# TensorE's order tied to the program's from the first step on, transposes included, with new places for chunk 2's attention

## The chip, the core and the metric

The kernel runs on one core of one Trainium2 chip. The metric is the device time of one execution in microseconds (us); lower is better. TensorE is called PE in the profile (its weight loads PEld), VectorE DVE, ScalarE ACT, GpSimd POOL and SyncE SP.

## The reference

Windowed attention over 8 sequences of 576 positions with 8 heads of 64, then a feed-forward network over the 4608 tokens:

```python
scores = scale * np.matmul(q, k.transpose(0, 1, 3, 2))      # scale = 1/8
mask = (rel >= 0) & (rel < 64)                              # rel = query - key
attn = softmax(np.where(mask, scores, -1e9))
x = np.matmul(attn, v)                                      # -> 4608 x 512
h = x @ w_in                                                # 512 -> 2048
g = h * np.tanh(log1p(exp(h)))
out = g @ w_out                                             # 2048 -> 512
```

## The kernel before, in words

The 4608 tokens are 12 chunks of 384 columns. Each chunk has an attention part for 4 pairs of heads, and a feed-forward part of 16 steps f.

The attention of one pair has three units on PE. **S**, the scores (`att_scores`): 12 small matmuls into two banks `s_ps`, one for each head. DVE then takes the masked minimum (L150), ACT the exponential (L153), DVE divides by the sum (L161 to L163) and `pr` is ready. **T**, the transposes (`att_transpose`): for chunks 0 to 3, two times three PE transposes of `pr` into `t_ps`, which ACT and DVE copy to `pT` (L185); from chunk 4 on DVE and DMAs do this, and PE has no T. **O**, the values (`att_values`): 12 small matmuls into `o_ps`, from which ACT and DVE make the split x (`xh`, `xl`, L205 and L206).

One feed-forward step of chunk c, written (c,f), is an **h unit** (12 matmuls into `h_ps`, of which there are two buffers), then min, Exp, Square, Ln, Exp and a product on DVE (L223, L233) and ACT, then `gh` and `gl` (POOL, and ACT for chunk 0), and two steps later an **acc unit** of 9 matmuls (`ffn_out`). A buffer of `h_ps` is free again when L233 has read it.

While chunk 0 runs, the weights are loaded and split into high and low parts (`load_w`, two calls after each step of chunk 0): L273 and L279 on ACT, L276, L277, L278 on DVE, L274 and L280 shared between DVE and POOL. The buffers `wa` of this work and `t` of the feed-forward steps share one ring of four.

The steps: first (0,0) to (0,7), then (0,8), (1,0), (0,9), (1,1) and so on to (0,15), (1,7), then (1,8) to (1,15), then the chunks 2 to 11 one after the other. The attention of chunk c+1 is set among the steps before its own by `plan`, which gives each S, T and O a place counted in half steps. `run` emits what has come due.

What sets the order on each engine is a scheduler that goes by the order of the program, by priorities (`tc.high_priority`) and by its own estimate of when things are ready. `in_order()` limits it: while it is active, each PE instruction that its block emits must stand behind the last PE instruction recorded in `order`, so that blocks follow one another on PE as they are written. It works only when `ordered` is not empty.

Of the kernel before, what the change touches and what calls it, by code (L numbers as in the profile page):

```python
# [27 lines left out]
def tile_window_attn_mish_ffn(  # L28
# [10 lines left out]
    nc = tc.nc  # L39
    NPAIR, _, NT = qT.shape  # L40
# [6 lines left out]
    NM = NB // 2  # L47
# [12 lines left out]
    ident = const.tile([P, P], F32, name="ident")  # L60
# [13 lines left out]
    for j in range(2):  # L74
        m = const.tile([P, P], F32, name=f"mask{j}")
# [16 lines left out]
    order = []  # L92
    ordered = []
# [4 lines left out]
    def in_order():  # L98
        return tc.issue_after(order[-1]) if ordered else nullcontext()
# [6 lines left out]
    def bank(c, p, name):  # L106
        if c == 2 or (c == 0 and p % 2 == 0):
            return ps_acc.tile([P, CH], F32, name=name, tag=next(sums))
        return ps_at.tile([P, CH], F32, name=name, tag="at")
# [56 lines left out]
    def att_transpose(c, p, pr):  # L166
        pT = next(pTs)
        if c > 3:


            moved = []
            tr = ap_.tile([P, P // 32, HM, 32], F32, name="tr", tag="pr", bufs=2)
            nc.vector.transpose(tr.rearrange("p k j i -> p j k i"),
                                pr.rearrange("p j (k i) -> p j k i", i=32))
            for r in range(0, P, 32):
                for k in range(0, P, 32):
                    if 0 <= k - r % BLK <= BLK:
                        moved.append(nc.sync.dma_start(pT[k:k + 32, r // 32, :, :], tr[r:r + 32, k // 32, :, :]))  # L178
            return pT, moved
        for h in range(2):  # L180
            t_ps = (bank(c, p, "t_ps") if c else ps_h.tile([P, CH], F32, name="t_ps", tag="h_ps")
                    ).rearrange("p (m k) -> p m k", k=P)
            for m in range(NM):
                nc.tensor.transpose(t_ps[:, m, :], pr[:, h * NM + m, :], ident)  # L184
            (nc.scalar.copy if h == 0 else nc.vector.tensor_copy)(  # L185
                pT[:, :, h * NM:(h + 1) * NM, :].rearrange("p r m i -> p m r i"),
                t_ps.rearrange("p m (r i) -> p m r i", i=32))
        return pT, []
# [19 lines left out]
    def ffn_in(c, x, f, alone=False):  # L208
        xh, xl = x
        h_ps = ps_h.tile([P, CH], F32, name="h_ps", tag="h_ps")  # L210
        n = 0
        for cc in range(NC_):
            for w, xx in ((wi_h, xh), (wi_h, xl), (wi_l, xh)):
                pe(h_ps, w[:, f, cc, :], xx[:, cc, :], start=n == 0, stop=n == 3 * NC_ - 1)
                n += 1
        t = mp.tile([P, CH], F32, name="t", tag="t", bufs=4)
        gh = mp.tile([P, CH], F32R, name="gh", bufs=3)
        gl = mp.tile([P, CH], F32R, name="gl", bufs=3)

        h = h_ps  # L220

        with tc.high_priority(offset=SOON):
            nc.vector.tensor_scalar(t, h_ps, 20.0, None, ALU.min)  # L223
            nc.scalar.activation(t, t, AF.Exp)  # L224
            if alone:

                h = ap_.tile([P, CH], F32, name="h", tag="pr", bufs=2)
                nc.scalar.copy(h, h_ps)
            nc.scalar.activation(t, t, AF.Square, bias=one_b)  # L229
            nc.scalar.activation(t, t, AF.Ln, bias=half_b, scale=0.5)  # L230
            nc.scalar.activation(t, t, AF.Exp, scale=-1.0)  # L231

            nc.vector.scalar_tensor_tensor(t, t, -1.0, h, ALU.add, ALU.mult)  # L233
            if c == 0:
                nc.scalar.copy(gh, t)  # L235
            else:
                nc.gpsimd.tensor_scalar(gh, t, 1.0, 0.0, ALU.mult, ALU.add)  # L237
            nc.gpsimd.tensor_tensor(gl, t, gh.bitcast(F32), ALU.subtract)  # L238
        return gh, gl
# [50 lines left out]
    class Att:  # L290
# [16 lines left out]
            self.load(p + 2, "qk")  # L307

        def transpose(self, p):
            self.pT[p] = att_transpose(self.c, p, self.pr.pop(p))  # L310

        def values(self, p):
            if self.x is None:
# [2 lines left out]
                att_values(self.c, p, self.v[p], self.pT.pop(p), self.x)  # L316
            self.load(p + 2, "v")

        def plan(self, begin, step, lag=1):

            for p in range(NPAIR):
                at = begin + p * step
                events.extend([(at, 2, self.scores, p), (at + 0.6 * step, 1, self.transpose, p),
                               (at + lag * step, 0, self.values, p)])

    events = []

    def run(slot):
        while events and events[0][0] <= slot:
            _, _, fn, p = events.pop(0)  # L330
            fn(p)
# [4 lines left out]
    def flush():  # L336
        c, f, gg = pend.pop(0)
        if f == 0:
            if c == 1:
                accs[c] = [ps_at.tile([P, DO], F32, name=f"acc1_{t}", tag="at") for t in range(NTT)]  # L340
            else:
                accs[c] = [ps_acc.tile([P, DO], F32, name=f"acc{t}", tag=f"acc{t}") for t in range(NTT)]
        ffn_out(accs[c], gg, f)
        if f == NF - 1:
            ffn_store(c, accs.pop(c))
# [6 lines left out]
    def take_w(n):  # L352
        for _ in range(min(n, len(todo_w))):
            w, f = todo_w.pop(0)
            w(f)
# [8 lines left out]
    third = 2 * len(steps) + 2  # L364
    steps += [(1, f) for f in range(NF - HEAD, NF)]
    starts = {c: 2 * len(steps) + 2 * NF * (c - 2) for c in range(2, NCHUNK)}
    steps += [(c, f) for c in range(2, NCHUNK) for f in range(NF)]

    atts = [Att(c) for c in range(NCHUNK)]
# [14 lines left out]
            take_w(1)  # L384
    take_w(1)
    atts[1].plan(0, 2 * HEAD / (NPAIR + 1))
    atts[2].plan(third, (starts[2] - third) / (NPAIR + 1), 1.5)


    ahead = 6  # L390
    begin = starts[2] + ahead + 1
    for c in range(3, NCHUNK):
        atts[c].plan(begin, (starts[c] - ahead - begin) / NPAIR)
        begin = starts[c] - ahead
    events.sort(key=lambda e: e[:2])
    for n, (c, f) in enumerate(steps):
        if f == 0:

            while any(fn.__self__ is atts[c] for _, _, fn, _ in events):
                run(events[0][0])  # L400
        if c == 2 and f == 0:
            ordered.append(True)
        with in_order():
            pend.append((c, f, ffn_in(c, atts[c].x, f, c == NCHUNK - 1)))
        run(2 * n)
        if len(pend) > LAG:
            with in_order():
                flush()
        run(2 * n + 1)
        if c == 0:  # L410
            take_w(2)
# [38 lines left out]
```

## Time and profile before

| what | value |
|---|---|
| time, median of 3 runs | 980.29 us (980.14 to 981.95) |
| the profiled execution: time, span | 981.9 us, 980.1 us |
| PE busy | 932.2 us, 95% of the span |
| PEld, DVE, ACT, POOL busy | 825.7, 490.5, 624.7, 327.2 us |
| mean granted TensorE clock | 0.973 of full |

Busy is the time in which an engine has an instruction under way, and matmuls overlap, so a busy PE can still be slow: its clock is sometimes granted at half. A row of the timeline reads: start in us, duration of the group in us, engine, line, operation, tiles as out<-in, count, and in brackets how long the engine had been idle before it and what ended the idle time. A score or value matmul in 32-bit floats shows as two records, so a whole S or O has 24 records in the trace and 12 rows in the program.

### The profile page before, as it was taken

Reading aid. Unit: us, or ns where it says so; the run is one execution under the profiler, and the core shown is the slowest. Engines: PE = TensorE matmul, PEld = TensorE weight load, DVE = VectorE, ACT = ScalarE, POOL = GpSimd, SP = SyncE. Lnnn points to the kernel's source line nnn. Section 1 sums busy time; section 2 is a strip of 40 time slices with the busy share of each in tenths; the row PEclk is TensorE's granted clock in tenths of the full one; section 3 lists DMA queues with packets and bytes.
Section 4 is the critical chain, followed back from the end, with each engine's and each line's share of the span. In section 5 each row is a group of like instructions: output and inputs, shape, how many; then the busy total and the mean of one; then the engine's idle time right before and its main releaser. Section 6 shows DMA issues by size and latency. Waiting matters only on the chain.

```text
span 980.1 us, 18009 instructions
## 1 busy us (share of the span) xinstructions
PE 932.2 (95%) x6432; PEld 825.7 (84%) x6432; DVE 490.5 (50%) x1352; ACT 624.7 (64%) x1529; POOL 327.2 (33%) x419
## 2 busy tenths in 40 slices
PE   4797779998999999999999999999999999999997
PEld 3586679987888898898888889889889889889996
DVE  6799965344444444454454454454454454453222
ACT  5677676664666666666666666666666666665664
POOL 2243454321333333333333333333333333333333
PEclk9787889998999999999999999999999999999999
DMA  7555430112212322322222221221221221210000
GB/s 243 191 174 170 142 106 1 50 43 75 74 51 72 94 68 55 93 69 55 89 74 55 83 80 54 84 81 53 84 81 53 83 81 53 85 29 13 33 1 33
DMA packets 80345, 76.16 MB, mean 78 GB/s; under 512 B 9600, under 2 KB 71552, under 8 KB 80256
## 3 DMA queue, kind: packets, MB, share of 16 engines
q1 hardware_dynamic: 80256, 75.01, 25.3%
q8 instruction: 51, 0.84, 0.4%
q14 instruction: 38, 0.31, 0.1%
HBM read 56.10 MB, written 9.44 MB: 67 GB/s over the span
## 4 chain that ended last, share of the span: by engine, by line
PE 85%; DVE 6%; DMA 3%; ACT 3%; issue 2%; SPq 1%; POOL 0%; ACTq 0%; DVEq 0%; POOLq 0%
PE h_ps L96 39%; PE acc L96 38%; PE s_ps L96 4%; PE o_ps L96 4%; DMA st<-w_in 1%; DVE wa L278 1%; DVE wa L277 1%; DMA st<-w_out 1%; SPq L178 1%; ACT pr L153 1%; DVE wa L276 1%; PE t_ps L184 1%; DVE t L223 1%; DVE t L233 0%; ACT wa L273 0%
## 5 line engine op out<-in xcount | busy, mean ns | idle before, releaser
L224 ACT ACTIVATE t<-t 128x384 f32<-128x384 f32 x192 | 100.4, 524 | 273.7 <-DVE t L223 273.5
L96 PE MATMUL h_ps<-xh,wi_h 128*128 128x384 f32 x768 | 263.8, 344 | 11.4 <-DVE t L233 11.3
L237 POOL TENSOR_SCALAR gh<-t 128x384 fp32r<-128x384 f32 x176 | 90.2, 512 | 535.5 <-DVE t L233 513.8
L96 PE MATMUL h_ps<-xh,wi_l 128*128 128x384 f32 x768 | 262.3, 342 | 0.0
L96 PE MATMUL h_ps<-xl,wi_h 128*128 128x384 f32 x768 | 262.2, 341 | 0.0
L96 PE MATMUL acc<-wo_h,gh 128*128 128x512 f32 x576 | 229.2, 398 | 0.9 <-POOL gh L237 0.9
L96 PE MATMUL acc<-wo_l,gh 128*128 128x512 f32 x576 | 226.0, 392 | 0.0
L233 DVE SCALAR_TENSOR_TENSOR t<-t,h_ps 128x384 f32<-128x384 f32 x176 | 97.2, 553 | 244.0 <-ACT t L231 239.1
L238 POOL TENSOR_TENSOR gl<-t,gh 128x384 fp32r<-128x384 f32 x192 | 197.6, 1029 | 30.8 <-ACT gh L235 16.2
L96 PE MATMUL acc<-wo_h,gl 128*128 128x512 f32 x576 | 204.6, 392 | 0.0
L96 PEld LDWEIGHTS h_ps<-xh,wi_h 128*128 128x128 f32 x768 | 147.4, 192 | 21.2 <-DVE t L233 12.4
L96 PEld LDWEIGHTS h_ps<-xl,wi_h 128*128 128x128 f32 x768 | 147.5, 192 | 7.5 <-issue 0.3
L96 PEld LDWEIGHTS h_ps<-xh,wi_l 128*128 128x128 f32 x768 | 147.5, 192 | 0.3 <-issue 0.2
L223 DVE TENSOR_SCALAR t<-h_ps 128x384 f32<-128x384 f32 x192 | 106.4, 555 | 71.8 <-PE h_ps L96 70.1
L96 PEld LDWEIGHTS acc<-wo_h,gh 128*128 128x128 f32 x576 | 108.7, 189 | 23.8 <-issue 6.0
L96 PEld LDWEIGHTS acc<-wo_h,gl 128*128 128x128 f32 x576 | 107.9, 188 | 22.8 <-issue 0.2
L96 PEld LDWEIGHTS acc<-wo_l,gh 128*128 128x128 f32 x576 | 108.5, 188 | 16.5
L230 ACT ACTIVATE t<-t,half_b 128x384 f32<-128x384 f32 x192 | 118.2, 616 | 5.7
L229 ACT ACTIVATE t<-t,one_b 128x384 f32<-128x384 f32 x192 | 118.3, 616 | 4.3
L153 ACT ACTIVATE pr<-pr,mx 128x128 f32<-128x128 f32 x288 | 111.5, 389 | 11.2 <-DVE mx L150 11.0
L231 ACT ACTIVATE t<-t 128x384 f32<-128x384 f32 x192 | 99.9, 521 | 4.5
L150 DVE CUSTOM_DVE_ANT_0 pr<-s_ps,mask 128x128 f32<-128x128 f32 x288 | 64.8, 285 | 15.9 <-PE s_ps L96 15.8
(49 smaller groups left out, 686.3 us busy)
## 6 DMA issues: line engine op xcount, KB each, us to landing
v_t<-vN SPq DMA_DIRECT2D x48, 384.0 KB, 3.8
k_t<-kT SPq DMA_DIRECT2D x47, 224.0 KB, 3.7
out<-o SPq DMA_DIRECT2D x36, 256.0 KB, 2.3
pT<-tr SPq DMA_DIRECT2D x384, 24.0 KB, 1.8
q_t<-qT SPq DMA_DIRECT2D x47, 192.0 KB, 3.7
st<-w_in SPq DMA_DIRECT2D x16, 512.0 KB, 4.2
st<-w_out SPq DMA_DIRECT2D x16, 512.0 KB, 3.4
q_t<-qT SPq DMA_DIRECT2D x3, 64.0 KB, 2.0
```

What stands on the lines that cost most here:

```text
L96: order.append(nc.tensor.matmul(*args, **kw).ins)
L150: nc.vector.tensor_tensor_reduce(out=pr[:, j, :], in0=s_ps[h][:, m, :], in1=mk, op0=ALU.add, op1=ALU.min, scale=-0.125, scalar=3.0e38, acc ...
L153: nc.scalar.activation(pr[:, j, :], pr[:, j, :], AF.Exp, bias=mx[:, j:j + 1], scale=-1.0, accum_out=sm[:, j:j + 1])
L178: moved.append(nc.sync.dma_start(pT[k:k + 32, r // 32, :, :], tr[r:r + 32, k // 32, :, :]))
L223: nc.vector.tensor_scalar(t, h_ps, 20.0, None, ALU.min)
L224: nc.scalar.activation(t, t, AF.Exp)
L229: nc.scalar.activation(t, t, AF.Square, bias=one_b)
L230: nc.scalar.activation(t, t, AF.Ln, bias=half_b, scale=0.5)
L231: nc.scalar.activation(t, t, AF.Exp, scale=-1.0)
L233: nc.vector.scalar_tensor_tensor(t, t, -1.0, h, ALU.add, ALU.mult)
L237: nc.gpsimd.tensor_scalar(gh, t, 1.0, 0.0, ALU.mult, ALU.add)
L238: nc.gpsimd.tensor_tensor(gl, t, gh.bitcast(F32), ALU.subtract)
```

## The change

`in_order()` becomes active before the first step (0,0) and no longer at step (2,0); transposes are recorded in `order` and are bound by `in_order()` like the other PE units; and for chunk 2 the place of T moves from 0.6 to 1.0 of the distance between two pairs. No instruction is added or removed.

```diff
             for m in range(NM):
-                nc.tensor.transpose(t_ps[:, m, :], pr[:, h * NM + m, :], ident)
+                order.append(nc.tensor.transpose(t_ps[:, m, :], pr[:, h * NM + m, :], ident).ins)
...
         def transpose(self, p):
-            self.pT[p] = att_transpose(self.c, p, self.pr.pop(p))
+            with in_order():
+                self.pT[p] = att_transpose(self.c, p, self.pr.pop(p))
...
-        def plan(self, begin, step, lag=1):
+        def plan(self, begin, step, turn=0.6, lag=1):
...
-                events.extend([(at, 2, self.scores, p), (at + 0.6 * step, 1, self.transpose, p),
+                events.extend([(at, 2, self.scores, p), (at + turn * step, 1, self.transpose, p),
...
-    atts[2].plan(third, (starts[2] - third) / (NPAIR + 1), 1.5)
+    atts[2].plan(third, (starts[2] - third) / (NPAIR + 1), 1, 1.5)
...
     events.sort(key=lambda e: e[:2])
+    ordered.append(True)
...
-        if c == 2 and f == 0:
-            ordered.append(True)
```

What this does to the order of the instructions is shown at three places. The number at the end of a tile's name tells the tiles apart: `h_ps_1129` belongs to step (0,8), `h_ps_996` to (0,6), `h_ps_1182` to (1,0), `h_ps_1215` to (0,9), `h_ps_1268` to (1,1), and `pr_933` to the last pair of chunk 1.

Place 1 is PE at the transposes of chunk 1's last pair. Before, they stand behind the h unit of (0,8), in the middle of an acc unit:

```order
L96 MATMUL h_ps_1129<-xh0_258,wi_l_103 128x384
L96 MATMUL acc0_679<-wo_h_104,gh_1010 128x512
L96 MATMUL acc0_679<-wo_l_105,gh_1010 128x512
L96 MATMUL acc1_680<-wo_h_104,gh_1010 128x512
L96 MATMUL acc1_680<-wo_l_105,gh_1010 128x512
L96 MATMUL acc2_681<-wo_h_104,gh_1010 128x512
L96 MATMUL acc2_681<-wo_l_105,gh_1010 128x512
L184 MATMUL t_ps_1020<-ident_77,pr_933 128x128 x3
L184 MATMUL t_ps_1025<-ident_77,pr_933 128x128 x3
```

Now they stand two steps earlier, right behind the h unit of (0,6), and the acc unit that follows is whole:

```order
L96 MATMUL h_ps_996<-xl0_259,wi_h_102 128x384
L96 MATMUL h_ps_996<-xh0_258,wi_l_103 128x384
L184 MATMUL t_ps_1020<-ident_77,pr_933 128x128 x3
L184 MATMUL t_ps_1025<-ident_77,pr_933 128x128 x3
L96 MATMUL acc0_679<-wo_h_104,gh_841 128x512
L96 MATMUL acc0_679<-wo_l_105,gh_841 128x512
L96 MATMUL acc0_679<-wo_h_104,gl_842 128x512
```

The transposes moved ahead of two h units and two acc units that stood before them.

Place 2 is DVE around the two products (L233) of steps (1,0) and (0,9), the reads that free both buffers of `h_ps`. Before:

```order
L223 TENSOR_SCALAR t_1195<-h_ps_1182 128x384
L223 TENSOR_SCALAR t_1228<-h_ps_1215 128x384
L274 TENSOR_SCALAR wa_1260<-wa_1260 128x512
L276 TENSOR_SCALAR wa_1260<-wa_1260 128x512
L276 TENSOR_SCALAR wa_1250<-wa_1250 128x512
L277 SCALAR_TENSOR_TENSOR wa_1260<-st_1258,wa_1260 128x512
L277 SCALAR_TENSOR_TENSOR wa_1250<-st_1248,wa_1250 128x512
L278 SCALAR_TENSOR_TENSOR wa_1260<-st_1258,wa_1260 128x512
L233 SCALAR_TENSOR_TENSOR t_1195<-t_1195,h_ps_1182 128x384
L233 SCALAR_TENSOR_TENSOR t_1228<-t_1228,h_ps_1215 128x384
```

Now:

```order
L278 SCALAR_TENSOR_TENSOR wa_1164<-st_1162,wa_1164 128x512
L233 SCALAR_TENSOR_TENSOR t_1195<-t_1195,h_ps_1182 128x384
L223 TENSOR_SCALAR t_1228<-h_ps_1215 128x384
L280 TENSOR_TENSOR wi_l_103<-wa_1164,wi_h_102 128x512
L274 TENSOR_SCALAR wa_1260<-wa_1260 128x512
L276 TENSOR_SCALAR wa_1260<-wa_1260 128x512
L223 TENSOR_SCALAR t_1281<-h_ps_1268 128x384
L277 SCALAR_TENSOR_TENSOR wa_1260<-st_1258,wa_1260 128x512
L233 SCALAR_TENSOR_TENSOR t_1228<-t_1228,h_ps_1215 128x384
```

The product of (1,0) moved ahead of the loads `wa_1260` and `wa_1250`, of the L223 of (0,9) and of one L280.

Place 3 is PE at chunk 2's attention. Before, the scores of its last pair stand in two halves around the transposes of the third, and two pairs end right behind one another before chunk 2's first h unit:

```order
L96 MATMUL s_ps<-k_t,q_t 64x128 x6
L184 MATMUL t_ps<-ident,pr 128x128 x6
L96 MATMUL s_ps<-k_t,q_t 64x128 x6
L96 MATMUL o_ps<-pT_106,v_t 64x64 x12
L184 MATMUL t_ps<-ident,pr 128x128 x6
L96 MATMUL o_ps<-pT_107,v_t 64x64 x12
L96 MATMUL h_ps<-xh_1973,wi_h 128x384
```

Now the same transposes and scores read:

```order
L96 MATMUL acc_2_1294<-wo_h,gl 128x512
L184 MATMUL t_ps<-ident,pr 128x128 x6
L96 MATMUL s_ps<-k_t,q_t 64x128 x12
L96 MATMUL h_ps<-xh_624,wi_h 128x384
L96 MATMUL h_ps<-xl_625,wi_h 128x384
```

The scores became whole, and a feed-forward unit stands between these units and what follows: behind this place come an h unit, the O of the third pair, an acc unit, an h unit, the T of the last pair, an acc unit, its O, and then chunk 2's first h unit. Of chunk 2's scores only the first pair's are still in halves, with one acc matmul between them.

SP's queue has the same 223 rows in both; around chunk 1's attention the loads of v, q and k and those of the weights change places with one another. On POOL some `wo_l` and `gl` rows change places.

## The prediction

> **What bounds the kernel now.** I read the page's first lines, then the span cut into stages, then PE's waits, then the timeline of each stage that the change touches.
>
> ```profile
> PE 932.2 (95%) x6432; PEld 825.7 (84%) x6432; DVE 490.5 (50%) x1352; ACT 624.7 (64%) x1529; POOL 327.2 (33%) x419
> PEclk9787889998999999999999999999999999999999
> ```
>
> ```profile
> 38.80:128.00 89.20, 68.38 (x445) 57.77 (x437) 79.28 (x170) 61.64 (x150) 32.80 (x29) 0.83 0.50 158
> 127.90:157.70 29.80, 29.74 (x141) 27.45 (x142) 22.19 (x37) 20.81 (x39) 16.32 (x16) 0.92 0.23 71
> 188.00:235.20 47.20, 43.96 (x364) 37.41 (x363) 22.55 (x83) 29.85 (x88) 12.19 (x16) 0.96 0.25 79
> 310.00:980.00 670.00, 664.13 (x4580) 593.82 (x4578) 294.65 (x831) 424.17 (x1024) 222.58 (x292) 1.00 0.22 63
> ```
>
> Each row of the second fence has the stretch and its length, then the busy time of PE, PEld, DVE, ACT and POOL, the granted clock, the DMA share and GB/s. From 310 on PE is busy 664 of 670 us at full clock, and the change only moves that stretch. In 38.8 to 128 DVE is busy 79.3 of 89.2 us and PE only 68.4, at 0.83 of its clock: here DVE, with the splitting of the weights, is the bound, and PE waits for it. From 128 on PE is the bound again, with a hole around chunk 2's attention (188 to 235). PE's waits over the whole span say the same:
>
> ```profile
> PE t_ps L184 <- DVE pr L163: 11.9, 3, 7.0
> PE h_ps L96 <- DVE t L233: 11.3, 2, 7.5
> ```
>
> Transposes wait for the divided `pr`, h units for the product that frees their buffer. I call the three stretches stage 1 (38.8 to 128), stage 2 (chunk 2's attention) and stage 3 (chunk 3's).
>
> **The price of a plain step.** In steps without attention PE goes from h unit to acc unit to h unit:
>
> ```profile
> 183.91 0.34 PE L96 MATMUL h_ps<-xh,wi_h 128*128 128x384 f32 x1
> 185.99 0.39 PE L96 MATMUL acc<-wo_h,gh 128*128 128x512 f32 x1
> 188.04 0.34 PE L96 MATMUL h_ps<-xh,wi_h 128*128 128x384 f32 x1
> ```
>
> An h unit takes 2.08 us, an acc unit 2.05, a step 4.13. The last row is the h unit of (1,13), and stage 2 begins with it.
>
> **Stage 1: when does PE become the bound?** In the order before, the h unit of (1,1) is the last to wait long; from it on PE has no hole until stage 2.
>
> ```profile
> 83.16 1.51 PE L184 MATMUL t_ps<-ident,pr 128*128 128x128 f32 x6 [7.04 <-DVE pr L163]
> 86.97 0.52 PE L96 MATMUL h_ps<-xl,wi_h 128*128 128x384 f32 x1
> 87.29 0.52 PE L96 MATMUL h_ps<-xh,wi_l 128*128 128x384 f32 x1
> 102.98 0.69 PE L96 MATMUL h_ps<-xh,wi_h 128*128 128x384 f32 x1 [3.83 <-DVE t L233]
> 127.96 0.69 PE L96 MATMUL h_ps<-xh,wi_h 128*128 128x384 f32 x1 [7.50 <-DVE t L233]
> ```
>
> Its start at 127.96 to 188.04 are 60.08 us for 14 steps, which at 4.13 make 57.8; the 2.3 over are matmuls at half clock after the wait (a pitch of 0.32 us, as in the two rows at 87, against 0.17 for an h unit of 2.08 us).
>
> That h unit starts when DVE has done the L233 of (1,0). Up to 38.8 us both orders are alike on DVE, so the start is 38.8 + the DVE work ahead of that L233 + DVE's idle time. Before: 89.2 = 79.3 + 9.9. The rows at the end of the stretch show what the new order takes out from in front of it:
>
> ```profile
> 121.20 1.01 DVE L223 TENSOR_SCALAR t<-h_ps 128x384 f32<-128x384 f32 x2
> 124.41 0.43 DVE L274 TENSOR_SCALAR wa<-wa 128x512 f32<-128x512 f32 x1 [2.19 <-ACT wa L273]
> 127.36 1.01 DVE L233 SCALAR_TENSOR_TENSOR t<-t,h_ps 128x384 f32<-128x384 f32 x2
> L280 DVE TENSOR_TENSOR wi_l<-wa,wi_h 128x512 fp32r<-128x512 f32 x9 | 7.3, 813 | 0.0
> ```
>
> The loads `wa_1260` and `wa_1250` from 124.41 to 127.36 (2.95 us), one of the two L223 (0.5) and one L280 (0.8, the mean of the stretch): 4.2 us. That leaves 75.1.
>
> DVE's idle time is the unknown. PE now stands at each T of chunk 1 until `pr` is ready, with everything behind it held; then T (1.5 us at half clock, row 83.16), an h or acc unit (12 times 0.32 = 3.8) and an O run, before DVE gets its next input (L206). DVE's own work in that time is one step's splitting, in the third pair for instance L274, L233, L185 and two each of L276, L277 and L278:
>
> ```profile
> L278 DVE SCALAR_TENSOR_TENSOR wa<-st,wa 128x512 uint32<-128x512 uint32 x19 | 16.6, 877 | 0.0
> L277 DVE SCALAR_TENSOR_TENSOR wa<-st,wa 128x512 uint32<-128x512 uint32 x20 | 15.6, 797 | 0.2
> L276 DVE TENSOR_SCALAR wa<-wa 128x512 uint32<-128x512 uint32 x20 | 13.3, 688 | 0.2
> 42.12 0.29 DVE L150 CUSTOM_DVE_ANT_0 pr<-s_ps,mask 128x128 f32<-128x128 f32 x1 [3.30 <-PE s_ps L96]
> 233.75 1.54 PE L96 MATMUL o_ps<-pT,v_t 128*64 128x64 f32 x22 [0.24 <-DVE pT L185]
> ```
>
> That is 0.4 + 0.5 + 0.5 + 2 times 2.4 = 6.2 us of work against 1.5 + 3.8 + 1.5 + 0.5 for ACT's copy = 7.3 us of PE: DVE idles about 1.2 us a pair. With four pairs (5), the idle 3.3 before the first scores (row 42.12, still there, since they follow O and h of the first step), and 1 to 2 us where (0,7) and (1,0) are late, idle time is again 10. Its bounds are 5 (PE at full clock behind every T, so only the 3.3 and the last term) and 25 (four times the whole path from T to S, below). I take 10, near the 9.9 measured. The h unit of (1,1) then starts at 38.8 + 75.1 + 10 = 123.9, 4.1 us earlier, and PE has run without a hole since the last T, so the 2.3 at half clock are gone. Against it: the 4.2 us of DVE work now lie in the next 29.8 us, where DVE was busy 22.2; at 26.4 of 28.9 (7 steps) it is nearly full, and an h unit will wait here and there: 1 us, between 0 and 4.2. Gain of stage 1: 4.1 + 2.3 - 1 = 5.4 us.
>
> **Stage 2: chunk 2's attention.**
>
> ```profile
> 192.27 0.89 PE L96 MATMUL s_ps<-k_t,q_t 64*64 64x128 f32 x24
> 193.09 0.45 PE L96 MATMUL h_ps<-xh,wi_h 128*128 128x384 f32 x1
> 198.81 0.87 PE L96 MATMUL s_ps<-k_t,q_t 64*64 64x128 f32 x12
> 199.62 0.45 PE L96 MATMUL h_ps<-xh,wi_l 128*128 128x384 f32 x1
> 206.35 0.92 PE L96 MATMUL o_ps<-pT,v_t 128*64 128x64 f32 x24
> 207.20 0.50 PE L96 MATMUL acc<-wo_l,gh 128*128 128x512 f32 x1
> 207.54 0.40 PE L96 MATMUL acc<-wo_h,gl 128*128 128x512 f32 x1
> 213.29 0.82 PE L184 MATMUL t_ps<-ident,pr 128*128 128x128 f32 x6
> 214.04 0.87 PE L96 MATMUL s_ps<-k_t,q_t 64*64 64x128 f32 x12
> 227.10 0.87 PE L96 MATMUL s_ps<-k_t,q_t 64*64 64x128 f32 x12 [0.24 <-ACT pT L185]
> 231.58 1.51 PE L184 MATMUL t_ps<-ident,pr 128*128 128x128 f32 x6 [2.76 <-DVE pr L163]
> 235.22 0.69 PE L96 MATMUL h_ps<-xh,wi_h 128*128 128x384 f32 x1
> ```
>
> A whole S (24 records) takes 193.09 - 192.27 = 0.82 us; half an S (12 records of one head) takes 0.81 as well. So each split costs a second 0.81. Changing between kinds of units costs 0.1 on each side (the first acc matmul after O takes 0.34 instead of 0.23). From 188.04 to 235.22 are 47.2 us with 7 steps (28.9) and 18.3 us of attention. After: the first S in halves 2.0; three times T and S together, 0.75 + 0.82 + 0.1 = 1.7 each; the last T 0.7; four O at 1.05: 12.0. T and S share three banks, so the S right behind a T waits for ACT's copy (0.24 in the row at 227.10): three times 0.3. No T should wait: `pr` is ready some 4 to 5 us after its S, and T now stands 7.2 us behind (acc, O, h, acc). 28.9 + 12.9 = 41.8: a gain of 5.4 us, from the 2.76 wait, two of the three splits and the half clock behind the wait.
>
> **Stage 3.** The half clock lasts into chunk 2's first step. Chunk 3's last O waits for the copies of a T that stands right ahead of it; now an acc unit stands between.
>
> ```profile
> 238.27 0.38 PE L96 MATMUL h_ps<-xh,wi_h 128*128 128x384 f32 x1
> 302.85 0.91 PE L96 MATMUL o_ps<-pT,v_t 128*64 128x64 f32 x22 [0.24 <-DVE pT L185]
> ```
>
> 235.22 to 238.27 are 9 matmuls in 3.05 us where 1.56 would do: 1.5 us; the two waits and a T in the midst of an acc unit make 0.5. Gain 2.0.
>
> **The sum.** 5.4 + 5.4 + 2.0 = 12.8 us. The profiled execution took 981.9 us (span 980.1, 1.8 around it), 1.6 above the median of 980.29; off its own time the sum gives 969.1, off the median 967.5. The moved DMA issues and POOL rows I cost at nothing: q, k and v are loaded two pairs ahead, and POOL is 33% busy with `gl` needed two steps later. Were that cover gone, a load's landing (3.7 us for `k_t`) per pair would show.
>
> ```profile
> k_t<-kT SPq DMA_DIRECT2D x47, 224.0 KB, 3.7
> ```
>
> [...] The trace shows half clock after a wait of 2.76 us, until 238.3. [...]
>
> **The rivals.**
> - *Stage 1 gives nothing* (20%): with strict order PE's waits only change places, DVE idles 14 us, (1,1) starts at 128 after a wait as before. 980.3 - 7.4 = 972.9.
> - *PE stays at full clock* (13%): the waits at T come out too short to bring half clock; PE then reaches O before DVE runs dry, idle time is 5 and (1,1) starts at 118.9: 9.1 + 2.3 - 1.5 + 7.4 = 17.3 gained, 963.
> - *Stage 2 keeps its hole* (10%): a T or S stands at its bank or at `pr` with the whole PE behind it. 980.3 - 5.4 - 2 = about 973.
> - *Slower* (6%): in stage 1 both engines wait in turn, DVE for O and S behind a held T, PE for `pr`. If DVE found nothing of its own to do, each pair would cost it T, h, O, copy and S: 1.5 + 3.8 + 1.5 + 0.5 + 1.6 = 8.9, four times 36; the start comes at 153 and the time at 996. It turns slower than before once DVE's idle time passes 26, about 5.6 us a pair. Against it: DVE has 6.2 us of work ready there.
> - *Nothing* (6%): the gains of the stages are taken back as holes between 128 and 188, where DVE gets fuller. 980.
>
> **How the numbers follow.** The forecast (967.5) has 45%, its own range being 964 to 972. To leave no more than 2 in 10 out, the range runs from 961 (the full-clock rival and a little) to 977 (stage 1 giving nothing and stage 2 half). A difference of 0.2% (2 us) is about what a measurement tells from none. Faster: 45 + 20 + 13 + 10 = 88%; same 6; slower 6.
>
> **What would show it.** Right: in the changed profile PE's last long wait for L233 before 130 us is gone and (1,1) starts near 124; T units wait for L163 before 105, followed by half clock; PE busy from then to 310 with waits under 1 us; all S but one of chunk 2 whole, chunk 2's first h unit near 224. Wrong: DVE idle over 20 us in stage 1, waits of h units for L233 between 125 and 185 adding to more than 4 us, or a wait of T for L163 in stage 2.

## The result, and the profile after

The changed kernel takes 966.13 us (median of 4 runs, 964.86 to 967.45), the kernel before beside it 980.21 (4 runs, 979.28 to 981.95): a ratio of 0.9854, with a 95% interval of 0.9835 to 0.9874. The profiled execution took 967.45 us with a span of 965.6, against 981.95 and 980.1 before: 14.5 us less from profile to profile, 14.1 from median to median. The forecast was 967.5, from a sum of 12.8.

The page's rows that answer to the first two shown of before, busy time and granted clock:

```profile
PE 918.2 (95%) x6432; PEld 813.7 (84%) x6432; DVE 489.0 (51%) x1352; ACT 624.5 (65%) x1529; POOL 330.4 (34%) x419
PEclk9679999999999999999999999999999999999999
```

PE is 14 us less busy with the same 6432 records. The mean granted clock (0.973 of 980.1 us before, 0.980 of 965.6 now) puts the time lost to half clock at 26.5 and 19.3 us, so half clock is about 7 of the 14; the page does not take the rest apart (units in pieces and units stretched around waits are among it). The low clock around 231 us (0.50 from 231.51 to 238.34 before) is gone; what is left lies in the first 101 us, but for the last 1.5 us of the span. The span of after cut at the same places of the program (a stretch and its length, busy time of PE, PEld, DVE, ACT, POOL, clock, DMA share, GB/s); the first stretch ends where the L233 of (1,0) does:

```profile
38.80:118.70 79.90, 60.27 (x427) 52.29 (x428) 70.66 (x161) 58.46 (x142) 32.09 (x28) 0.85 0.49 162
118.70:181.20 62.50, 59.94 (x298) 52.83 (x297) 37.20 (x60) 43.81 (x81) 30.72 (x31) 1.00 0.15 51
181.20:222.90 41.70, 41.70 (x364) 35.74 (x363) 22.20 (x83) 29.36 (x88) 11.39 (x14) 1.00 0.28 89
222.90:300.40 77.50, 77.50 (x581) 68.94 (x577) 37.23 (x118) 50.04 (x133) 24.07 (x32) 1.00 0.22 66
```

The third and fourth rows, chunk 2's and chunk 3's attention, are now without a hole: PE busy for all of them, at full clock. In the first row DVE is again the busiest, 70.7 of 79.9 us. PE's waits between 38 and 240 us (total, times, longest):

```profile
PE t_ps L184 <- DVE pr L163: 17.5, 3, 6.9
PE h_ps L96 <- DVE t L233: 3.2, 4, 1.1
PE t_ps L184 <- ACT t L224: 1.4, 1, 1.4
```

The h units no longer wait 11.3 us for L233; the T units wait 17.5 instead of 11.9 for L163. All four waits at T end by 96 us, three of them with a T at half clock (1.51 us for six transposes):

```profile
51.03 1.51 PE L184 MATMUL t_ps<-ident,pr 128*128 128x128 f32 x6 [5.17 <-DVE pr L163]
69.25 1.51 PE L184 MATMUL t_ps<-ident,pr 128*128 128x128 f32 x6 [6.90 <-DVE pr L163]
81.36 0.85 PE L184 MATMUL t_ps<-ident,pr 128*128 128x128 f32 x6 [1.36 <-ACT t L224]
95.80 1.51 PE L184 MATMUL t_ps<-ident,pr 128*128 128x128 f32 x6 [5.49 <-DVE pr L163]
```

The stages by their boundaries. An h unit is found by its place in PE's order, and its start is read in the trace. (The prediction calls the h unit at 188.04 "(1,13)"; it is that of (1,9). The count of 14 steps from (1,1) to it and of 7 in stage 2 was made for the right one.)

| us | (1,1) starts | to (1,9) | stage 2, to (2,0) | to (3,0) | to the span's end |
|---|---|---|---|---|---|
| before | 128.0 | 60.1 | 47.2 | 79.8 | 665.1 |
| after | 119.3 | 61.9 | 41.7 | 77.5 | 665.2 |
| difference | -8.6 | +1.8 | -5.5 | -2.3 | 0 |

In after the h unit of (1,1) no longer starts with a wait. These are the start of the h unit before it, that of (0,9), the L233 of (1,0), and the start of (1,1):

```profile
115.09 0.45 PE L96 MATMUL h_ps<-xh,wi_h 128*128 128x384 f32 x1 [0.72 <-DVE t L233]
118.19 0.54 DVE L233 SCALAR_TENSOR_TENSOR t<-t,h_ps 128x384 f32<-128x384 f32 x1
119.33 0.34 PE L96 MATMUL h_ps<-xh,wi_h 128*128 128x384 f32 x1
```

The L233 is done at 118.73, when PE is still at the acc unit ahead. From the last T (95.80) to 119.33 PE is busy for 22.8 of 23.5 us, so in the new order PE's own work and DVE's meet here, where before PE waited 7.5 us for DVE.

### The profile page after: what moved, and what is told of

Its sections match the earlier page's. It is cut to its first block, busy times and chain, and to the rows that moved or that the text cites. A ratio compares the mean times of both kernels' runs of the same rounds, so it can differ in the third digit from the quotient of the medians.

```text
span 965.6 us, 18005 instructions
## 1 busy us (share of the span) xinstructions
PE 918.2 (95%) x6432; PEld 813.7 (84%) x6432; DVE 489.0 (51%) x1352; ACT 624.5 (65%) x1529; POOL 330.4 (34%) x419
## 4 chain that ended last, share of the span: by engine, by line
PE 83%; DVE 6%; issue 3%; ACT 3%; DMA 3%; POOL 1%; SPq 1%; ACTq 0%; POOLq 0%; DVEq 0%
PE h_ps L96 38%; PE acc L96 37%; PE o_ps L96 4%; PE s_ps L96 3%; DMA st<-w_out 2%; DVE wa L277 1%; DVE wa L278 1%; ACT wa L273 1%; SPq L178 1%; POOL wo_l L280 1%; ACT pr L153 1%; DVE wi_l L280 1%; PE t_ps L184 1%; DVE pr L150 0%; DVE wa L276 0%
## 5 line engine op out<-in xcount | busy, mean ns | idle before, releaser
L96 PE MATMUL h_ps<-xh,wi_l 128*128 128x384 f32 x768 | 259.4, 338 | 0.0
L96 PE MATMUL h_ps<-xl,wi_h 128*128 128x384 f32 x768 | 259.2, 337 | 0.0
L233 DVE SCALAR_TENSOR_TENSOR t<-t,h_ps 128x384 f32<-128x384 f32 x176 | 97.3, 553 | 245.6 <-ACT t L231 240.7
L238 POOL TENSOR_TENSOR gl<-t,gh 128x384 fp32r<-128x384 f32 x192 | 199.0, 1036 | 38.6 <-ACT gh L235 24.0
L96 PEld LDWEIGHTS h_ps<-xh,wi_h 128*128 128x128 f32 x768 | 145.3, 189 | 13.5 <-DVE t L233 5.4
L96 PEld LDWEIGHTS h_ps<-xl,wi_h 128*128 128x128 f32 x768 | 145.3, 189 | 6.7
L96 PEld LDWEIGHTS h_ps<-xh,wi_l 128*128 128x128 f32 x768 | 145.4, 189 | 0.0
L223 DVE TENSOR_SCALAR t<-h_ps 128x384 f32<-128x384 f32 x192 | 106.5, 555 | 68.3 <-PE h_ps L96 64.8
```

Source lines behind the costliest of these rows:

```text
L96: order.append(nc.tensor.matmul(*args, **kw).ins)
```

## The experiments

Theory: the gain is in three places that hardly touch one another. Stage 1 is as long as DVE's time ahead of (1,1), stage 2 gets shorter because T moves away from its S and the units stay whole, and stage 3 mostly because no wait is left that brings half clock. Rivals: PE's strict order gains nothing in stage 1; the transposes in order are all of it; or a place of T alone (0.6 or 1.0) is. All stage tables are like the one above, from one profiled execution each; e2 and e4, whose stage 1 is that of the changed kernel, reach (1,1) at 117.4 and 118.1 where it has 119.3, so a start there is known to some 2 us. The ratios are as measured, and differ by up to 0.2% from the quotient of the two medians named.

### Parts of the change

`e1_no_transposes` is the kernel before with the order active from the start, and nothing else:

```diff
     events.sort(key=lambda e: e[:2])
+    ordered.append(True)
...
-        if c == 2 and f == 0:
-            ordered.append(True)
```

> One part alone: the order holds from the first step on, but transposes are neither recorded nor bound, and chunk 2's transposes keep their old place. Theory (DVE's order decides stage 1, whole scores and no hole decide stage 2): stage 1 gains as in the change, 6 to 7 us; in stage 2 two more scores are in halves and transposes cut into acc units, 2 to 3 us lost. About 968.5. Rival A (binding the transposes is what matters): most of the gain is gone, 975 or more.

`e2_turn_06` is the changed kernel with T of chunk 2 at its old place:

```diff
-    atts[2].plan(third, (starts[2] - third) / (NPAIR + 1), 1, 1.5)
+    atts[2].plan(third, (starts[2] - third) / (NPAIR + 1), 0.6, 1.5)
```

> The change with the old place (0.6) of chunk 2's transposes. Stage 1 is the same program. Theory: one more score in halves (0.8 us), and transposes 5 us behind their scores instead of 7, just about when pr is ready: 967 to 968. Rival B (the new place is what closes chunk 2's hole): a wait of 2 to 3 us with half clock behind it returns, 970 to 972.

`e3_from_1_8` is the changed kernel with the order active only from (1,8) on, so that stage 1 is as before:

```diff
-    ordered.append(True)
...
+        if c == 1 and f == HEAD:
+            ordered.append(True)
```

> The change, but the order holds only from step (1,8) on: stage 1 is the old program, stages 2 and 3 the new one. Theory: 980.2 less the 7.4 to 7.8 us of stages 2 and 3: 972.6, and the first h unit of chunk 2 comes about 6 us before 235.2. Rival C (stage 1 is bound by DVE's total work, so its order is worth nothing): nearly all of the gain, 967.

`e4_until_1_8` is the reverse, with T of chunk 2 at 0.6: order up to (1,8), none while chunk 2's attention runs:

```diff
+        if c == 1 and f == HEAD:
+            ordered.clear()
+        if c == 2 and f == 0:
+            ordered.append(True)
```

> The opposite: the order holds in stage 1 and again from step (2,0) on, but not from (1,8) to (2,0), and chunk 2's transposes keep their old place: stage 1 new, stage 2 old. Theory: 980.2 less 6.8 of stage 1 and 0.5 of stage 3: 973. Rival C: 979.5.

Measured, against 979.8 us for the kernel before in the same rounds (the changed kernel's row is from its own comparison):

| kernel | time (us) | ratio [95%] | (1,1) starts | to (1,9) | to (2,0) | to (3,0) |
|---|---|---|---|---|---|---|
| changed | 966.13 | 0.9854 [0.9835, 0.9874] | 119.3 | 61.9 | 41.7 | 77.5 |
| e1, no transposes in order | 969.02 | 0.9888 [0.9872, 0.9905] | 119.6 | 61.4 | 43.3 | 78.3 |
| e2, T at 0.6 | 967.57 | 0.9875 [0.9859, 0.9891] | 117.4 | 61.9 | 42.3 | 77.5 |
| e3, only from (1,8) | 972.98 | 0.9934 [0.9919, 0.9949] | 126.7 | 60.1 | 41.7 | 77.5 |
| e4, only until (1,8) | 974.0 | 0.994 [0.9924, 0.9957] | 118.1 | 61.9 | 46.4 | 78.5 |

The parts add up. e3 has stages 2 and 3 of the changed kernel to the tenth (41.7 and 77.5) without its stage 1, and takes 973: this is the number that the prediction gave for "stage 1 gives nothing". e4 has stage 1 without stage 2, and takes 974. They gain 6.8 and 5.8 of the 14.1 us, so neither is a by-product of the other; the 1.5 left over are within what one set of runs differs from the next (e4's four runs lie between 971.8 and 974.9, and the profiled one, which the table shows, is the fastest). Order for the matmuls alone (e1) has all of stage 1 and most of stage 2; the transposes in order and their later place are worth 2.9 us by the medians (969.02 to 966.13), 2.4 of them in stages 2 and 3 by the table. The place of T alone (e2) makes 0.6 us in stage 2, and the two times cannot be told apart.

What PE waited for between 38 and 240 us in e1:

```profile
PE o_ps L96 <- DVE pT L185: 7.2, 4, 4.1
PE h_ps L96 <- DVE t L233: 6.5, 4, 3.3
PE o_ps L96 <- ACT pT L185: 3.1, 4, 1.1
PE t_ps L184 <- ACT t L230: 2.1, 1, 2.1
```

Without the transposes in order the same DVE work is waited for at other units, O and h, and (1,1) starts at 119.6 all the same. So the total of PE's waits in stage 1 shows where PE stands when DVE is late, and not the length of the stage. Neither the transposes in order nor their place makes the gain of stage 1: it comes with the order of the other units, S, O, h and acc.

### Is DVE the bound of stage 1?

`e6_turn_1_chunk1` moves T and O of chunk 1 to later places as well (1.0 and 1.5), so that no T should stand waiting long for `pr`:

```diff
-    atts[1].plan(0, 2 * HEAD / (NPAIR + 1))
+    atts[1].plan(0, 2 * HEAD / (NPAIR + 1), 1, 1.5)
```

> The change with chunk 1's transposes and values also later (1.0 and 1.5 of the distance). PE's waits at the transposes of stage 1 (18.9 us in the changed profile) shrink to under 8. Theory (DVE bounds stage 1): the start of (1,1) moves by under 2.5 us, 964 to 968.5. Rival E (these waits are what stage 1 now costs): 5 us or more faster, 961 or less.

Measured: 966.13 us, ratio 0.9864 [0.9843, 0.9885], (1,1) at 119.6. The waits moved and the time stayed:

```profile
PE h_ps L96 <- DVE t L233: 12.0, 6, 5.3
PE t_ps L184 <- DVE pr L163: 4.8, 2, 2.9
```

17.5 us of waiting at T became 4.8, and 3.2 at the h units became 12.0.

`e7_light_before` and `e7_light_after` are both kernels without L277, one of DVE's splitting operations:

```diff
-        nc.vector.scalar_tensor_tensor(a, hi, 0xC0000000, a, ALU.bitwise_and, ALU.bitwise_or)
```

> The kernel before without L277, one of the five DVE operations of each weight split (its output has wrong weights). Theory (stage 1 is bound by DVE): 15 us of DVE work less in stage 1; the start of (1,1) comes 8 to 14 us earlier, 966 to 972. Rival F (stage 1 is bound by the order in which PE waits): 977 or more.

> The changed kernel without L277, likewise. Theory: 13 us of DVE work less; the start of (1,1) comes 6 to 11 us earlier, 955 to 960; the gap between the two light kernels is 9 to 14 us, mostly stages 2 and 3. Rival F: 964 or more.

Measured against 981.06: light before 963.27 (0.9834 [0.9811, 0.9856]), faster than its range of 966 to 972, and light after 957.63 (0.9773 [0.975, 0.9796]), within its own. Of the expected distance of 9 to 14 us between the two only 5.6 is left. Stage 1 of both, to the start of (1,1):

```profile
38.80:110.80 72.00, 56.70 (x419) 48.95 (x418) 61.21 (x139) 57.17 (x140) 32.31 (x30) 0.93 0.55 184
38.80:112.50 73.70, 58.18 (x423) 50.06 (x421) 59.27 (x146) 58.81 (x145) 29.96 (x28) 0.88 0.54 178
```

The first row is light before, the second light after. With L277 gone, DVE is idle for 10.8 and 14.4 us, and the order before reaches (1,1) 1.7 us earlier than the new one, not 8.6 later. That DVE's work counts is shown: (1,1) came 17.1 and 6.8 us earlier with one DVE operation gone. But the two are not alike. In the light kernel of the new order PE's order around chunk 1's attention is that of the changed kernel, unit by unit, and DVE is busy for 12.0 us less up to (1,1) (59.3 for 71.3), of which only 6.8 are gained: there DVE is no longer the one bound.

The light kernel of the order before is in neither order. Nothing binds PE in its stage 1, and without L277 the scheduler wrote another one: T of chunk 1's last pair stands one step earlier, two S that were in halves are whole, and on DVE the L223 of (0,9) stands behind the L233 of (1,0), as in the changed kernel. That L233 ends at 107.53, and (1,1) starts at 110.82 without a wait. So the 17.1 us hold a change of order beside the lighter DVE, and it is not shown that the advantage of the new order is there only while DVE is full.

### Why was DVE's time shorter than worked out?

The prediction left 75.1 us of DVE work ahead of (1,1); it was 70.7. The group of after in stage 1 that had changed most, beside two that had not:

```profile
L276 DVE TENSOR_SCALAR wa<-wa 128x512 uint32<-128x512 uint32 x18 | 8.0, 464 | 0.1
L277 DVE SCALAR_TENSOR_TENSOR wa<-st,wa 128x512 uint32<-128x512 uint32 x18 | 13.5, 764 | 0.1
L278 DVE SCALAR_TENSOR_TENSOR wa<-st,wa 128x512 uint32<-128x512 uint32 x18 | 15.4, 867 | 0.1
```

L276 took 464 ns on the mean, where the same instruction took 688 before. The timeline of the kernel before shows why one is long: DVE and POOL at two moments.

```profile
66.78 0.42 DVE L276 TENSOR_SCALAR wa<-wa 128x512 uint32<-128x512 uint32 x1
90.23 1.44 POOL L280 TENSOR_TENSOR wo_l<-wa,wo_h 128x512 fp32r<-128x512 f32 x1 [3.21 <-ACT wo_h L279]
90.46 1.76 DVE L278 SCALAR_TENSOR_TENSOR wa<-st,wa 128x512 uint32<-128x512 uint32 x1
91.63 1.45 POOL L238 TENSOR_TENSOR gl<-t,gh 128x384 fp32r<-128x384 f32 x1
92.14 1.23 DVE L276 TENSOR_SCALAR wa<-wa 128x512 uint32<-128x512 uint32 x1
```

With POOL idle L276 takes 0.42 us. At 92.14 it starts while POOL's L238 is under way and ends at 93.37, 0.29 after it; the L278 above it ends 0.55 after POOL's L280. Of the 20 L276 of stage 1 before, ten met no POOL instruction, and took 0.42; five of the other ten took 1.2 to 1.5. Taking each DVE operation against the median of its own line alone, those that overlapped with POOL took DVE some 15 us more before and 10 after, of which POOL's L280 (the low part of w_out) makes about 7 and 4 to 5 (some operations met two POOL instructions). L223 and L233, which read `h_ps`, took 0.55 with or without POOL. So in this trace 0.42 us became up to 1.5 beside POOL; no row shows what in the chip makes it so.

`e9_light_pool_before` and `e9_light_pool_after` test whether POOL is the cause by taking L280 off POOL:

```diff
-        (nc.vector if first else nc.gpsimd).tensor_tensor(wl, af, wh.bitcast(F32), ALU.subtract)
+        if first:
+            nc.vector.tensor_tensor(wl, af, wh.bitcast(F32), ALU.subtract)
...
+        if f == 0:
+            nc.gpsimd.memset(wo_l.bitcast(F32), 0.0)
```

> The kernel before, without POOL's subtraction for w_out's low part (L280 on POOL, 1.48 us each; the low part is zero instead, so that the product with it adds nothing; its matmuls run as before). DVE's instructions are the same. Theory (DVE's splitting operations wait for POOL where the two overlap): the 7.5 us by which DVE's operations beside POOL's L280 were longer than the same ones alone go from stage 1; L276's mean falls from 688 to under 600 ns, (1,1) starts near 121 instead of 128, and the time is about 974 (970 to 977). Rival (a long L276 is its own matter, as of its operands): L276, L277 and L278 keep their means within 30 ns, (1,1) stays at 127 to 129, and the time at 980.

> The same left out of the changed kernel. Theory: 4.0 us of stage 1's DVE time lay in overlaps with POOL's L280, so (1,1) starts near 115.5 instead of 119.3, and the time is about 962.5 (960 to 965); the distance between the two orders at (1,1) falls from 8.6 to about 5. Rival: no change, 966, and the distance stays 8.6.

Measured against 979.94: 978.53 (0.9987 [0.9968, 1.0006]) and 973.73 (0.9941 [0.9921, 0.9961]). By the times the theory failed, which had 974 and 962.5, for a reason that lies in the edit: the scheduler put the memset of `wo_l` at the very start of POOL, ahead of the mask, and the first scores' softmax waits for that.

```profile
3.49 6.92 POOL L289 MEMSET wo_l<- 128x8192 f32 x1
10.48 0.64 POOL L70 TENSOR_SCALAR_AFFINE_SELECT mask<-mask 64x128 f32<-64x128 f32 x2
```

So (0,0) starts at 45.5 and 47.1 us instead of 35.9 and 38.7. Counted from (0,0) to (1,1), stage 1 answers the question. The four windows in the order before, after, light-pool before, light-pool after:

```profile
35.90:128.00 92.10, 71.28 (x453) 60.23 (x452) 82.18 (x175) 62.80 (x151) 32.80 (x29) 0.82 0.49 155
38.70:119.30 80.60, 60.98 (x430) 52.91 (x430) 71.26 (x162) 58.77 (x143) 32.79 (x28) 0.85 0.49 163
45.50:126.90 81.40, 68.05 (x452) 57.42 (x451) 68.88 (x164) 59.34 (x146) 19.03 (x19) 0.87 0.49 159
47.10:128.10 81.00, 60.77 (x431) 52.71 (x431) 68.14 (x162) 58.53 (x144) 18.48 (x20) 0.85 0.49 157
```

The order before loses 13.3 us of DVE time and 10.7 us of length when POOL's L280 is gone; the new order loses 3.1 of DVE time and nothing of its length. L276's mean fell to 504 ns in the one (from 688), and did not fall in the other (508, from 464); L163's mean fell from 1344 and 1337 ns to 950 and 959. Without L280 the two orders are equally long from (0,0) to (1,1), 81.4 and 81.0, where 92.1 and 80.6 stood with it. So the theory holds for the durations. For the new order it failed in the time: PE's order around chunk 1's attention is that of the changed kernel, the last T comes 56.9 us after (0,0) instead of 57.1, and the shorter DVE operations gained nothing. For the order before the 10.7 is no clean price: the late start shifts which loads have been done by (0,0), and here too the scheduler, which nothing binds in this stage, wrote another order (T of chunk 1's last pair stands behind a whole acc unit, and the L233 of (1,0) and (0,9) are no longer side by side).

### A version that beats both?

`e8_later_loads` takes four of the loads' turns later, out of stage 1:

```diff
-            take_w(2)
+            take_w(1 if 2 <= f < 6 else 3 if f >= HEAD else 2)
```

> The changed kernel with four of the weight loads (about 2.9 us of DVE work each) taken one or two steps' turn later: one load instead of two beside chunk 0's steps 2 to 5, three instead of two from step 8 on. Theory (stage 1 is as long as DVE's work ahead of (1,1), and nothing else there binds): three loads fewer stand ahead of (1,1) on DVE, 8 us, so (1,1) starts at about 112 instead of 119.3; some of it is paid back behind it, where DVE has 10 loads instead of 7 to do in eight units. Time about 961, between 957 and 966. Rival (PE's own order, T behind the softmax, is what is left of stage 1): (1,1) moves by less than 3 us and the time stays at 964 to 968.

Measured: 972.43 us, 0.9927 [0.991, 0.9943]: slower than the changed kernel by 6.3. Stage 1 behaved as the theory has it, if less strongly: (1,1) starts at 114.8 instead of 119.3, 4.5 us for 7.1 us less of DVE work (64.1 for 71.3). But from there to (1,9) are 71.9 us instead of 61.9. The window behind (1,1) and the waits that cost it:

```profile
114.80:153.60 38.80, 30.63 (x126) 27.34 (x127) 34.37 (x50) 24.65 (x47) 19.55 (x19) 0.83 0.34 108
114.81 0.69 PE L96 MATMUL h_ps<-xh,wi_h 128*128 128x384 f32 x1 [6.04 <-DVE t L233]
128.22 0.44 PE L96 MATMUL h_ps<-xh,wi_h 128*128 128x384 f32 x1 [2.12 <-DVE t L233]
142.81 0.69 PE L96 MATMUL h_ps<-xh,wi_h 128*128 128x384 f32 x1 [6.04 <-DVE t L233]
```

DVE is busy 34.4 of 38.8 us there: the loads, moved late, make DVE the bound of the next stretch, and the two waits of 6 us each bring half clock (the clock of the window is 0.83). The expectation allowed "some of it" to be paid back, and had 957 to 966 us; it was 10.0 for 4.5. No version run here beats the changed kernel beyond the measurement while doing the same work.

### Score matmuls, two heads side by side

The prediction priced a split S, with another unit between its halves, at a second 0.81 us. `e5_heads_apart` tests what an S costs when its heads stand one after the other with nothing between:

```diff
-        for m in range(NM):
-            for par, h in ((0, 0), (1, 1), (1, 0), (0, 1)):
+        for h, m, par in itertools.product(range(2), range(NM), range(2)):
```

> The change with every pair's scores written one head after the other instead of in turn (the same 12 matmuls). It prices a split. Theory (half of a unit takes as long as the whole, 0.81 us, because only the matmuls of two heads side by side overlap): 0.8 us for each of the 40 units from chunk 2 on that count, 32 us: about 998. Rival D (the 0.81 us of a half was a wait for its bank or a lack of weight loads ahead): under 5 us, 966 to 971.

Measured: 982.01 us, ratio to the kernel before 1.002 [1.0007, 1.0032], 15.9 us above the changed kernel where 32 were expected. To exclude that the heads had been mixed after all, `e11_heads_apart` sets each head's six matmuls in an ordered block of its own:

```diff
+        for h in range(2):
+          with in_order():
+            for m, par in itertools.product(range(NM), range(2)):
```

> The changed kernel with each head's six score matmuls in a row of their own, first those of one head and then those of the other, so that no two heads stand beside each other in PE's row. If the two heads of a pair run beside each other in PE (12 matmuls in 0.81 us, as six take alone), a half of S takes about 1.6 us instead of 0.8, each pair 1.6 us more, and with some 40 pairs on PE's path behind (1,1) the time is about 1030 (1015 to 1040); the S rows of 24 matmuls last over 2 us. If the array takes one matmul after another in any order, nothing changes: 966.

Measured: 981.59, 1.0016 [1.0003, 1.003]. PE's rows are the same in both (six of one head, then six of the other) but for one place, so e11 is e5 again, and the expected 1030 was far off. The one place is chunk 2's first S, which has an acc matmul between its halves in e5 and is whole in e11; stage 2 lasts 41.7 us in e5 and 40.9 in e11. One S of e11 and what follows it, and one of the changed kernel:

```profile
407.74 1.15 PE L96 MATMUL s_ps<-k_t,q_t 64*64 64x128 f32 x24
408.82 0.50 PE L96 MATMUL acc<-wo_h,gh 128*128 128x512 f32 x1
```

```profile
418.04 0.89 PE L96 MATMUL s_ps<-k_t,q_t 64*64 64x128 f32 x24
418.85 0.50 PE L96 MATMUL acc<-wo_h,gh 128*128 128x512 f32 x1
```

1.08 us against 0.81: a price of 0.27 for heads that follow one another, not of 0.8. A true split is another matter: the one S that e11 made whole saved 0.7 us of stage 2. In the single records of the S of e11, head one's six matmuls start at 0, 0.16, 0.27, 0.38, 0.49 and 0.60 us, and head two's first at 0.28, beside head one's third, although the program has three more matmuls of head one between the two. So these matmuls did not start in the order of the program. With 32 S from (3,0) on 0.27 makes 8.6 of the 9.1 us by which e5 is longer there (674.3 against 665.2). Of the rest 3.8 us lie ahead of (1,1), which starts at 123.1, and 2.1 from there to (3,0).

## Why the prediction was right

The time was right (966.13 for 967.5), the three terms less so: two of the sizes in stage 1 were off, in opposite directions, and part of the agreement there is luck. Stages 2 and 3 came out with their mechanism.

- **Start of (1,1): 123.9 predicted, 119.3 measured.** The mis-sized term is DVE's work ahead of it, 75.1 us predicted and 70.7 measured. Of the 8.6 us less than before some 5.3 are shorter overlaps with POOL (15.2 and 9.9 us), which the prediction did not have; 3.3 are left for the moved work. The prediction used the durations of the trace of before as if they were the operations' own. They held overlaps with POOL's instructions in them, as e9 shows for L280 (13.3 us of DVE time less without it in the order before), and the new order lets L276 meet POOL in 4 cases of 18 instead of 10 of 20. Why the new order moves just these apart, I can't say; no run here places a single POOL instruction.
- **DVE's idle time: 10 predicted, 9.2 measured, largely by luck.** The sum had 5 of it from four pairs in which PE is held at T and starves DVE. The trace has one wait of DVE for PE in the whole stretch, the 3 us near its start that the sum had as well; 6.1 of the 9.2 us are waits for ACT. These are the largest:

```profile
DVE t L223 <- PE h_ps L96: 3.0, 1, 3.0
DVE wi_l L280 <- ACT wi_h L279: 2.1, 3, 1.2
DVE wa L274 <- ACT wa L273: 1.6, 3, 1.0
```

- **(1,1) starts when the L233 of (1,0) is done.** So it was before; in the changed kernel the L233 is done 0.6 us earlier than PE gets there.
- **Two bounds of the working.** The upper bound of DVE's idle time, 25 us as "four times the whole path", is 36 by the path's own sum (8.9 us). And by the prediction's terms the change turns slower once DVE idles for 22.8 us (14.1 + 2.3 - 1 + 7.4), not 26. Neither enters the forecast.
- **The moved DVE work, 4.2 us, as a gain.** Its price is not shown by itself. That all of stage 1's gain comes from the order there is shown (e3 lacks it and is some 7 us slower); which moved instruction earns it is argued. With DVE relieved (e7, e9) the new order is no earlier at (1,1) than the old one, measured from 38.8 us or from (0,0), but the old one is then in another order.
- **From (1,1) to (1,9): 58.8 predicted, 61.9 measured.** 14 steps make 57.8. The half clock of 2.3 us did go, as predicted (clock 1.00 in the window). The catch-up term, 1 us, measured 4.1: three waits of h units for L233 (2.4 us, the longest 1.12), and 1.7 by which units are stretched, all of it in the first six steps behind (1,1); it is at the end of the bound of 0 to 4.2 that stood beside it. Together with (1,1) stage 1 gave 6.8 us for 5.4.
- **Stage 2: 41.8 predicted, 41.7 measured.** Its parts stood up: three whole S, one in halves, no wait of a T, and each S right behind a T stretched from 0.89 to 1.18 us, where the sum had 0.3 for the bank:

```profile
191.57 0.82 PE L184 MATMUL t_ps<-ident,pr 128*128 128x128 f32 x6
192.32 1.18 PE L96 MATMUL s_ps<-k_t,q_t 64*64 64x128 f32 x24
197.76 0.92 PE L96 MATMUL o_ps<-pT,v_t 128*64 128x64 f32 x24
200.80 0.82 PE L184 MATMUL t_ps<-ident,pr 128*128 128x128 f32 x6
201.55 1.18 PE L96 MATMUL s_ps<-k_t,q_t 64*64 64x128 f32 x24
```

- **Stage 3: 2.0 predicted, 2.3 measured.** e3, with the same stage 2, has the same 77.5. Both parts of the sum show: e4 keeps a long wait of a T for `pr` (20.1 us in four between 38 and 240 us, where the changed kernel has 17.5 in three) and has 78.5; e1 has no such wait, but its transposes stand free, and it has 78.3.
- **The signs named beforehand.** The long wait for L233 before 130 us is gone, and (1,1) starts at 119.3, not near 124. T waits for L163 before 105 us and half clock follows: yes. PE's waits under 1 us from (1,1) to 310: nearly, one of 1.12 at 124.75. Chunk 2's first h unit near 224: 222.9. The h units' waits for L233 stayed under the 4 us that would have spoken against it (in all 3.2 us, one of them just ahead of (1,1)).
- **The rivals.** "Stage 1 gives nothing" named 972.9, which is e3's time, where stage 1 is left as it was; for the change itself it did not come true. "PE stays at full clock" had (1,1) at 118.9, near the 119.3 measured, but by another mechanism than the one that happened: the waits at T were long and the half clock behind them was there.
- **Half clock behind a wait.** Half clock followed each of the waits of 5.2, 6.9 and 5.5 us at T, as it did behind the long waits before, and none of those of 1.4 us and less. That it followed a wait of 2.76 us, as the prediction read in the trace, stands (the granted clock of before is 0.50 from 231.51 to 238.34). But the length of a wait alone does not tell. Half clock followed a wait of 2.12 us in the kernel before (the wait for T that ends at 47.09), and not one of the same 2.12 us in e8 (the row at 128.22). In the traces of before and after the granted clock changes only at moments that are whole multiples of 3.41 us apart; here are two stretches of that length of before and of e8, the one with the wait (or its first part) and the next, before first:

```profile
43.78:47.19 3.41, 1.29 (x8) 0.87 (x7) 2.67 (x7) 3.41 (x11) 0.61 (x1) 1.00 0.54 185
47.19:50.60 3.41, 3.18 (x20) 2.36 (x20) 3.38 (x8) 3.07 (x8) 0.00 (x0) 0.50 0.00 0
124.22:127.63 3.41, 1.88 (x9) 1.21 (x7) 2.15 (x5) 3.38 (x8) 1.27 (x1) 1.00 0.56 181
127.63:131.04 3.41, 2.82 (x15) 2.73 (x16) 2.31 (x4) 3.03 (x6) 2.19 (x3) 1.00 0.31 126
```

In the kernel before, the wait lies within one such window and leaves PE idle for 2.12 of its 3.41 us; in e8 it is divided into 1.53 and 0.59.

## What to carry to other kernels

Where an engine is full, price the change of order by what its operations cost alone, and look in the timeline for what ran beside them: a mean of the trace holds the company that the old order gave it. Where PE waits is no measure of the length of such a stage: e1 and e6 moved over 12 us of PE's waits from T to other units, and (1,1) started at the same time. A test kernel in which nothing binds the order may come out in another order than the one it is to test (the light kernels of the order before did): compare the orders before the times. And work moved behind a full stretch comes back with interest if the next stretch has no room for it: e8 gained 4.5 us and paid 10.

## What the runs showed of the hardware

- DVE's splitting operations took longer in a part of their overlaps with a POOL instruction. In stage 1 of the kernel before L276 took 0.42 us in the ten cases that met none, and 1.2 to 1.5 in five of the ten that met one; L163 took 1.34 us on the mean there and 0.95 in e9, without POOL's L280. L223 and L233, which read `h_ps`, took 0.55 us either way.
- Two heads' score matmuls, each on 64 rows of the array in the records, ran side by side. In the S of the changed kernel at 418.04, where they stand in turn, the matmuls start in twos, within 0.02 us of each other, and the twelve take 0.81 us, as the six of one head alone do in the kernel before (198.81). In the S of e11 at 407.74, where one head's six all stand ahead of the other's, the second head started 0.28 us after the first, and the twelve took 1.08 us: 0.27 more than in turn.
- The granted clock changes only on a grid of 3.41 us in the traces of before and after, whose place differs between the two (before at 47.19 and 57.43, after at 49.31 and 56.14). From 36 to 250 us the two have 105 such windows at full clock. Each of the eight in which PE idled for 2.12 us or more was followed by half clock; of the other 97, in which it idled for 1.82 us at most, none was. This half clock lasted for two or three windows, 6.8 or 10.2 us.
